# Sums as a column of ones among the values, in an attention and experts kernel

## The chip, the core and the metric

The kernel runs on one core of a Trainium2 chip. The metric is the device time of one execution in microseconds, the median of several runs.

## The reference

Two stages follow each other. The first is attention with 32 memory slots per head; the second sends each token to one of eight experts.

```python
# 8 batches, 8 heads, 576 tokens, head size 64, 32 slots; all float32
a = exp(phi - max_over_tokens(phi)); a = a / (sum_over_tokens(a) + 1e-9)
k_m = einsum('bhsm,bhsd->bhmd', a, k)          # memory keys
v_m = einsum('bhsm,bhsd->bhmd', a, v)          # memory values
attn = softmax(q @ k_m.T / 8); x = attn @ v_m  # 4608 tokens of 512
logits = x @ w_gate + modality_bias[modality_id]
e = argmax(logits); g = softmax(logits)[e]
out = g * (relu(x @ w1[e]) @ w2[e])            # 512 -> 1024 -> 512
```

The sum over tokens of `a`, one number for each head and slot, is what the change works out in another way.

## The kernel before

**Staging.** The kernel guesses one expert from the modality bias and computes all tokens with it. A verdict at the end (`verdict`, line 741) tells whether any token preferred another; only then a second part (`again`, line 1317, a branch on a register) does the work for all experts. With these inputs the branch skips it. The eight batches are worked off in turn, two of them to a pair. The value side of attention is folded into the first expert matrix: `value_products` (line 750) multiplies memory values by `w1`, `hidden` (814) multiplies the attention weights by that, `relu` (827 and 831) brings the result back in two parts, high and low, and `outputs` (850) does the second expert matrix in 24 matmuls of 512 columns for each tile of 128 tokens. `gated` (863) scales a tile on ACT into one of two `ob` buffers, and `store` sends it out from SP's queue.

**The memory of a batch.** `mem_max` to `mem_peak` find the maximum of phi, `mem_exp` (385 and 388) subtracts it on DVE and takes exponentials on ACT in two parts. From batch 1 on, `mem_sums` adds the nine token columns of the exponentials on GpSimd in a tree of four additions (`fold`, lines 311 to 315), and `kv_products` multiplies the exponentials by keys and values: 72 products of 64 rows, 32 columns of weights and 128 moving columns (64 of keys, 64 of values), in 144 instructions on tiles of the array, and one more product of the sums with `sides` (line 425), which adds over partitions. `kv_divide` divides on ACT, `mem_turn` turns keys and values for the next steps. Batch 0 has its own path (`first_products`, `first_sums`), with its sums on DVE.

**Loads.** Keys and values of a batch lie side by side in `kv_sb`, each loaded with one DMA in runs of 2,304 bytes. `more_keys`, behind the memory product, issues the next batch's. `load_queries` issues 16 DMAs in runs of 128 bytes. Nearly all DMAs go out from SP's queue, in order.

**The order.** Every engine executes its instructions in the order in which the code emits them. `weave` (line 1207) works that order out when the kernel is built: a list of attention stages, each with a due time, is woven into a list of expert stages. `TAKES` holds planned durations for each kind of stage (PE first, then a chain of engines such as "D0.4 A0.6"), `progress` counts expert work in about microseconds, and a stage is emitted once its predecessors are planned to be done and progress has reached its due time. Attention stages are strictly in order of due time. For the sums there is an allowance:

```python
t = max([0.0] + [done[n] + (0.1 if n[0] != "sums" else -1.2) for n in s[0][2] if n[0] != "g"])
```

The due times that matter here, after the start of a batch's memory work: `exp` 3.0, `sums` 3.2, the four query transpositions 5.6 to 8.6, logits of the batch before and `kv` at `MEMORY` (6.0), `kvT` 9.0.

**The end.** The last tile is evicted in halves, one on ACT and one on DVE, and stored with four DMAs, two from SP and two from ACT. Then each engine loads the verdict into a register (`values_load`, line 1408) and branches (line 1318).

Of the kernel before, what the change touches and what calls it, by code (L numbers as in the profile page):

```python
# [54 lines left out]
def attn_moe(ctx: ExitStack, tc: tile.TileContext, q, k, v, phi, mod_id, w_gate, mod_bias, w1, w2, out):  # L55
# [23 lines left out]
    BUSY = 145, 9  # L79
# [24 lines left out]
    sides = const.tile([P, NG], F32, name="sides")  # L104
# [25 lines left out]
    kv_sb = big.tile([P, 2, HG, QC * D], F32, name="kv_sb")  # L130
# [3 lines left out]
    raw2 = kv_sb.rearrange("p t j x -> p (t j x)")[:, 0:FCH * DM].rearrange("p (c d) -> p c d", d=DM)  # L134
# [28 lines left out]
    def warm_small(n):  # L163
        idle = pair_of_banks(0)
        for n in range(n):
            r, c = QP * (n % 2), BL * (n // 2 % 4)
            nc.tensor.matmul(
                idle[c:c + BL, n % 2, 0:16], lhsT=busy[r:r + QP, 0:BL], rhs=busy[r:r + QP, 0:16],
                start=True, stop=True, tile_position=(r, c),
            )  # L170
# [7 lines left out]
    def load_kv(b, t):  # L178
        nc.sync.dma_start(kv_sb[:, t], halves((k, v)[t], b))
# [128 lines left out]
    def fold(eng, src, op, name, where):  # L308

        t2 = wk.tile([P, HG, 4 * M], F32, name="t2" + where)  # L310
        eng.tensor_tensor(t2, src[:, :, 0:4 * M], src[:, :, 4 * M:8 * M], op=op)
        eng.tensor_tensor(t2[:, :, 0:2 * M], t2[:, :, 0:2 * M], t2[:, :, 2 * M:4 * M], op=op)
        r = wk.tile([P, HG, M], F32, name=name, bufs=2 if name == "sums" else 1)
# [12 lines left out]
    def mem_max(b):  # L326
        live["top", b] = fold(nc.vector, phs[b % 2], ALU.max, "top", "top")
# [39 lines left out]
    def mem_exp(b):  # L367
# [21 lines left out]
        live["pe", b] = pe, None  # L389

    def mem_sums(b):
        pe = live["pe", b][0]
        if b == 0:
            x = pe.rearrange("p j x -> p (j x)")
            n = QC // 3 * P
            t2 = wk.tile([P, HG, 4 * M], F32, name="t2top").rearrange("p j x -> p (j x)")[:, 0:n]
            r = wk.tile([P, HG, M], F32, name="sums", bufs=2)
            rf = r.rearrange("p j m -> p (j m)")
            nc.vector.tensor_tensor(t2, x[:, 0:n], x[:, n:2 * n], op=ALU.add)
            nc.vector.tensor_tensor(t2, t2, x[:, 2 * n:3 * n], op=ALU.add)  # L400
            nc.vector.tensor_tensor(rf, t2[:, 0:P], t2[:, P:2 * P], op=ALU.add)
            nc.vector.tensor_tensor(rf, rf, t2[:, 2 * P:3 * P], op=ALU.add)
            live["pe", b] = pe, r
            return
        live["pe", b] = pe, fold(nc.gpsimd, pe, ALU.add, "sums", "sums")
        if b > 1 and b + 2 < B:
            load_phi(b + 2)

    def kv_products(b):


        pe, sums = live["pe", b]
# [12 lines left out]
        nc.tensor.matmul(live["psum"], lhsT=sums.rearrange("p j m -> p (j m)"), rhs=sides, start=True, stop=True)  # L425

    def first_products(t):
# [9 lines left out]
        for c in range(QC):  # L437
            for j, g, half in tiles:
                nc.tensor.matmul(  # L439
                    to[g][M * j:M * (j + 2), 0:2 * D].rearrange("p (j d) -> p j d", j=2),  # L440
                    lhsT=pe[half, c, j:j + 2].rearrange("p j m -> p (j m)"), rhs=kv_sb[half, t, j:j + 2, c * D:(c + 1) * D],
                    start=(c == 0), stop=(c == QC - 1), tile_position=(QP * g, M * j),
                )
# [52 lines left out]
    def kv_divide(b):  # L496
# [6 lines left out]
        for g in range(NG):  # L503
            nc.scalar.activation(both[:, :, g], live["kvp"][:, g], AF.Copy, scale=rec[:, g])
        live["both", b] = both

    def more_keys(b):
        if b == 0:
            load_kv(1, 0)
            load_kv(1, 1)  # L510
            load_queries(1)
            load_modalities()
        elif b == 1:
            load_phi(2)
            load_phi(3)
        if 0 < b < B - 1:
            load_kv(b + 1, 0)
            load_kv(b + 1, 1)
# [23 lines left out]

    def mem_gate(b):
        pg = bank("pe" if b > 1 else "pa")
# [202 lines left out]


# [117 lines left out]
    def store(b, t):  # L866
# [6 lines left out]
        def finish(po):  # L873
            if b == B - 1 and t is None:
                parts = []
                for n, eng in enumerate((nc.sync, nc.scalar)):
                    ob = wk.tile([P, DM], F32, name="ob", bufs=2)
                    cols = slice(DM // 2 * n, DM // 2 * (n + 1))
                    if n:
                        nc.vector.tensor_scalar(ob[:, cols], po[:, cols], gate_of(b, t), None, op0=ALU.mult)  # L880
                    else:
                        nc.scalar.activation(ob[:, cols], po[:, cols], AF.Copy, scale=gate_of(b, t))
                    parts.append((eng, ob, cols))
# [21 lines left out]
    def first_w2(c):  # L905
# [44 lines left out]
    def plan_memory(b, due, floor=0.0):  # L950
# [6 lines left out]
        for name, after, what, late in (  # L957
# [3 lines left out]
            ("sums", [("exp0" if b < 2 else "exp", b)], mem_sums, 3.2),  # L961
            ("kv", [("exp0" if b < 2 else "exp", b), ("sums", b)], mem_kv, 6.0),
# [99 lines left out]
    def plan_steps(b, dues):  # L1062
# [46 lines left out]
        if b > 1:  # L1109
            add(("l", b), "lx", [("n", b, 1, 2), ("s", b, 0)] + ([("exp", b + 1), ("sums", b + 1)] if b + 1 < B else []), logits, b)  # L1110
# [80 lines left out]
    FIRST, AHEAD, SPREAD, MEMORY, LATE = 26.5, (1.4, 4.0), 0.55, 6.0, 4  # L1191
# [87 lines left out]
    with tc.manual_schedule():  # L1279
# [15 lines left out]
        nc.gpsimd.memset(sides, 0.0)  # L1295
        for g in range(NG):
            nc.gpsimd.memset(sides[QP * g:QP * (g + 1), g:g + 1], 1.0)
# [109 lines left out]
    why = "one or zero, worked out on the chip"  # L1407
    again(nc.values_load(bad_i[0:1, 0:1], min_val=0, max_val=P, skip_runtime_bounds_check_because=why))
# [28 lines left out]
```

## Time and profile before

| | us |
|---|---|
| median of 3 runs | 387.86 (387.04 to 390.87) |
| the profiled execution | 387.67 |
| its span, first to last instruction | 385.9 |
| PE busy | 373.8 |
| VectorE (DVE) busy | 247.7 |
| ScalarE (ACT) busy | 140.1 |
| GpSimd (POOL) busy | 47.4 |

The difference between the profiled execution's time and its span, 1.8 us, lies before the first and behind the last instruction. The mean granted clock of TensorE was 0.994. PE stands for matmuls and PEld for weight loads, which overlap them; a q behind an engine (ACTq, SPq) is its sequencer, which issues DMAs and does register work. Ends of matmuls are modelled, so starts are the better guide. An L with a number is a line of the kernel before.

### The profile page before, as it was taken

The page shows a single profiled execution, that of the slowest core. Times are in us where ns is not written, and L with a number is a line of the kernel's source. Part 1 is how long each engine was busy: PE and PEld are TensorE (multiplying, and loading weights), DVE is VectorE, ACT ScalarE, POOL GpSimd, SP SyncE. Part 2 cuts the span into 40 slices and gives each one's busy share as a digit, 9 for nine tenths or more (in the row PEclk, how much of TensorE's full clock was granted, in tenths as well). Part 3 has the DMA queues.
Part 4 walks back from the last instruction along what each step waited for, and adds up shares of the span by engine and source line. Part 5 has one row for each costly group of instructions (what it writes and reads, how often), then busy time and mean ns, then how long its engine had stood idle before and what let it go on. Part 6 is the DMA issues. An engine that isn't in the chain of part 4 may idle for free.

```text
span 385.9 us, 9650 instructions
## 1 busy us (share of the span) xinstructions
PE 373.8 (97%) x3878; PEld 304.4 (79%) x3879; DVE 247.7 (64%) x620; ACT 140.1 (36%) x327; POOL 47.4 (12%) x123
## 2 busy tenths in 40 slices
PE   7899999999999999999999999999999999999992
PEld 3577886879769887987879887887968877888981
DVE  4786756796688568856776468865796458850400
ACT  2382424515245235423443234331543225341310
POOL 4237050023000300030000300030000300000000
PEclk9999999999999999999999999999999999999997
DMA  8998679794951594729601395607001000420011
GB/s 297 376 400 196 72 132 336 166 303 127 291 126 29 161 252 98 279 63 296 128 27 56 76 304 107 278 24 273 32 27 54 3 29 27 189 114 35 23 56 34
DMA packets 94762, 56.87 MB, mean 147 GB/s; under 512 B 72564, under 2 KB 77940, under 8 KB 94708
## 3 DMA queue, kind: packets, MB, share of 16 engines
q1 hardware_dynamic: 94272, 55.74, 48.1%
q8 instruction: 32, 0.52, 0.5%
q10 hardware_dynamic: 436, 0.43, 0.4%
q14 instruction: 22, 0.18, 0.2%
HBM read 37.28 MB, written 18.87 MB: 146 GB/s over the span
## 4 chain that ended last, share of the span: by engine, by line
PE 90%; DVE 5%; ACT 2%; DMA 1%; issue 1%; ACTq 0%; POOL 0%; DVEq 0%; POOLq 0%
PE pe L850 50%; PE pe L814 26%; PE pair L420 4%; PE pair L568 2%; PE pe L757 2%; PE pair L757 1%; PE pair L703 1%; DMA row<-n_moe_modality_bias_dram 1%; PE pair L584 1%; PE pair L425 1%; PE pair L149 1%; PE pe L439 1%; DVE a L623 1%; DVE a L617 0%; DVE mx L621 0%
## 5 line engine op out<-in xcount | busy, mean ns | idle before, releaser
L850 PE MATMUL pe<-w2h,hh 128*128 128x512 f32 x288 | 115.6, 401 | 0.0
L850 PE MATMUL pe<-w2h,hl 128*128 128x512 f32 x288 | 112.4, 390 | 0.0
L850 PE MATMUL pe<-w2l,hh 128*128 128x512 f32 x288 | 110.1, 390 | 0.0
L831 DVE SCALAR_TENSOR_TENSOR hl<-pe,hh 128x256 fp32r<-128x256 f32 (+2 forms) x158 | 58.0, 391 | 37.4 <-ACT hh L827 36.5
L850 PEld LDWEIGHTS pe<-w2h,hh 128*128 128x128 f32 x288 | 54.1, 188 | 16.4 <-ACT vwh L154 4.2
L827 ACT ACTIVATE hh<-pe 128x256 fp32r<-128x256 f32 (+2 forms) x158 | 53.4, 363 | 36.9 <-PE pe L814 36.4
L850 PEld LDWEIGHTS pe<-w2l,hh 128*128 128x128 f32 x288 | 54.0, 188 | 11.6
L850 PEld LDWEIGHTS pe<-w2h,hl 128*128 128x128 f32 x288 | 54.2, 188 | 9.6
L863 ACT ACTIVATE ob<-pe,gates 128x512 f32<-128x512 f32 x35 | 24.0, 689 | 79.0 <-PE pe L850 37.8
L814 PE MATMUL pe<-xbh,vwh 128*128 128x320 f32 x128 | 39.9, 312 | 0.1
L814 PE MATMUL pe<-xbl,vwh 128*128 128x320 f32 x128 | 39.6, 309 | 0.0
L814 PE MATMUL pe<-xbh,vwl 128*128 128x320 f32 x128 | 39.6, 309 | 0.0
L814 PE MATMUL pe<-xah,vwh 128*128 128x256 f32 x124 | 35.2, 287 | 0.6 <-ACT xah L683 0.4
L814 PE MATMUL pe<-xal,vwh 128*128 128x256 f32 x124 | 35.0, 284 | 0.3 <-DVE xal L686 0.3
L814 PE MATMUL pe<-xah,vwl 128*128 128x256 f32 x124 | 34.9, 283 | 0.0
L354 POOL COPY ts<-tm 32x4 f32<-32x4 f32 x24 | 4.8, 200 | 184.4 <-DVE tm L346 183.6
L814 PEld LDWEIGHTS pe<-xah,vwh 128*128 128x128 f32 x124 | 23.5, 191 | 3.1 <-ACT xah L683 1.3
L814 PEld LDWEIGHTS pe<-xbh,vwh 128*128 128x128 f32 x128 | 24.0, 188 | 0.7 <-ACT ob L863 0.4
L814 PEld LDWEIGHTS pe<-xbl,vwh 128*128 128x128 f32 x128 | 24.1, 188 | 0.3
L814 PEld LDWEIGHTS pe<-xal,vwh 128*128 128x128 f32 x124 | 23.6, 191 | 0.8 <-DVE xal L686 0.5
L814 PEld LDWEIGHTS pe<-xbh,vwl 128*128 128x128 f32 x128 | 24.0, 188 | 0.0
L814 PEld LDWEIGHTS pe<-xah,vwl 128*128 128x128 f32 x124 | 23.6, 191 | 0.0
(184 smaller groups left out, 438.2 us busy)
## 6 DMA issues: line engine op xcount, KB each, us to landing
kv_sb<-in_k_dram SPq DMA_DIRECT2D x8, 1152.0 KB, 5.9
kv_sb<-in_v_dram SPq DMA_DIRECT2D x8, 1152.0 KB, 9.1
q_sb<-in_q_dram SPq DMA_DIRECT2D x112, 72.0 KB, 2.4
out_dram<-ob SPq DMA_DIRECT2D x28, 256.0 KB, 2.7
ph<-in_phi_dram SPq DMA_DIRECT2D x7, 576.0 KB, 4.2
raw<-in_moe_w_dram SPq DMA_DIRECT2D x2, 1024.0 KB, 6.2
out_dram<-ob SPq DMA_DIRECT2D x14, 128.0 KB, 2.3
raw<-in_moe_w_dram SPq DMA_DIRECT2D x1, 1280.0 KB, 10.0
```

The lines of the kernel that those rows point to most:

```text
L149: nc.tensor.transpose(dst, src, ident[:rows, :rows])
L354: nc.gpsimd.tensor_copy(ts_[BL * a:BL * (a + 1)], live["tm"][BL * o:BL * (o + 1)])
L420: nc.tensor.matmul(live["kvp"][M * j:M * (j + 1), g], lhsT=pe[half, j, c * M:(c + 1) * M], rhs=kv_sb[half, :, j, c * D:(c + 1) * D], start ...
L425: nc.tensor.matmul(live["psum"], lhsT=sums.rearrange("p j m -> p (j m)"), rhs=sides, start=True, stop=True)
L439: nc.tensor.matmul(to[g][M * j:M * (j + 2), 0:2 * D].rearrange("p (j d) -> p j d", j=2), lhsT=pe[half, c, j:j + 2].rearrange("p j m -> p ( ...
L568: nc.tensor.matmul(sc[g][M * j:M * (j + 1), a, 0:QC * BL].rearrange("p (c t) -> p c t", t=BL), lhsT=kvTs[b][half, 0, j], rhs=qT[half, j, a ...
L757: nc.tensor.matmul(pvs[g][M * j:M * (j + 1), :], lhsT=vT[b][rows, j, :], rhs=raw1[rows, j, cols], start=True, stop=not more, tile_position ...
L814: nc.tensor.matmul(ph[:, 0:n], lhsT=(vl if k == 2 else vh)[:, g, cols], rhs=xl if k == 1 else xh, start=(g == k == 0), stop=(g == NG - 1 a ...
L827: nc.scalar.activation(hs[0][:, f, h0:h0 + p1 - p0], live["ph", f][:, p0:p1], AF.Relu)
L831: nc.vector.scalar_tensor_tensor(hl, live["ph", f][:, p0:p1], 0.0, hh.bitcast(F32), op0=ALU.max, op1=ALU.subtract)
L850: nc.tensor.matmul(po, lhsT=tile_columns(hl if n == 1 else hh, f, t), rhs=(w2l if n == 2 else w2h)[:, f, :], start=(f == n == 0), stop=(f ...
L863: nc.scalar.activation(ob, po, AF.Copy, scale=gate_of(b, t))
```

## The change

The sums come out of the memory product itself. Each 64 values in `kv_sb` are followed by a one, set by one GpSimd memset ahead of batch 1's loads; the moving operand becomes two runs of 65 numbers, keys (with one number too many, which nobody reads) and values with their one, so that column 129 of the result is the sum. GpSimd's tree, `sides` and the product of line 425 go. Values from batch 1 on are loaded with four DMAs, in runs of 64 numbers. The load of phi two batches ahead is issued behind the exponentials. In the plan the memory product and the logits follow the exponentials alone, the product is planned at 2.3 for 2.6, and `MEMORY` is 7.4 for batches 3 to 7. Batch 1's gate becomes eight products on tiles of 64 rows, with 14 small filler products. The last tile is evicted by ACT alone and stored with two DMAs. The verdict is loaded into the registers during the last tiles.

```diff
-    BUSY = 145, 9
+    BUSY = 145, 9, 14
...
-    sides = const.tile([P, NG], F32, name="sides")
...
-    kv_sb = big.tile([P, 2, HG, QC * D], F32, name="kv_sb")
+    ks = QC * D
+    kv_sb = big.tile([P, HG, ks + QC * (D + 1)], F32, name="kv_sb")
+    with_ones = kv_sb[:, :, ks:].rearrange("p j (c e) -> p j c e", e=D + 1)
...
     def load_kv(b, t):
-        nc.sync.dma_start(kv_sb[:, t], halves((k, v)[t], b))
+        src = halves((k, v)[t], b)
+        if b == 0 or t == 0:
+            nc.sync.dma_start(kv_sb[:, :, ks * t:ks * (t + 1)], src)
+            return
+        for j in range(HG):
+            nc.sync.dma_start(with_ones[:, j, :, 0:D], src[:, j].rearrange("p (c d) -> p c d", d=D))
...
         live["pe", b] = pe, None
+        if 1 < b < B - 2:
+            load_phi(b + 2)
...
-        live["pe", b] = pe, fold(nc.gpsimd, pe, ALU.add, "sums", "sums")
-        if b > 1 and b + 2 < B:
-            load_phi(b + 2)
+    def keys_and_values(half, j, c):
+
+        x = kv_sb[half, j, c * D:c * D + D + 1]
+        return bass.AP(tensor=x.tensor, offset=x.offset, ap=[list(x.ap[0]), [ks + c, 2], [1, D + 1]])
...
-        pk = pair_of_banks(1)
-        live["psum"] = pk[:, 0, 2 * D:2 * D + NG]
-        live["kvp"] = pk[:, :, 0:2 * D].rearrange("p g (t d) -> p g t d", t=2)
+        pk = pair_of_banks(1)[:, :, 0:2 * (D + 1)]
+        live["psum"] = pk[:, :, 2 * D + 1]
+        live["kvp"] = pk.rearrange("p g (t e) -> p g t e", t=2)
...
-                        rhs=kv_sb[half, :, j, c * D:(c + 1) * D],
+                        rhs=keys_and_values(half, j, c),
...
-        nc.tensor.matmul(live["psum"], lhsT=sums.rearrange("p j m -> p (j m)"), rhs=sides, start=True, stop=True)
...
     def more_keys(b):
         if b == 0:
+            nc.gpsimd.memset(with_ones[:, :, :, D], 1.0)
             load_kv(1, 0)
...
+    def second_gate():
+
+        pg = pair_of_banks(0)
+        for j in range(HG):
+            for g in range(NG):
+                half = slice(QP * g, QP * (g + 1))
+                nc.tensor.matmul(
+                    pg[M * j:M * (j + 1), g, 0:E], lhsT=vT[1][half, j], rhs=wgd[half, j, g],
+                    start=True, stop=True, tile_position=(QP * g, M * j),
+                )
+        small_products(BUSY[2], pg[:, :, QP:QP + 16])
+        nc.vector.tensor_copy(vg[0][:, :, E:2 * E], pg[:, :, 0:E])
...
+    def count_bad():
+        why = "one or zero, worked out on the chip"
+        live["bad"] = nc.values_load(bad_i[0:1, 0:1], min_val=0, max_val=P, skip_runtime_bounds_check_because=why)
...
             if b == B - 1 and t is None:
-                parts = []
-                for n, eng in enumerate((nc.sync, nc.scalar)):
-                    ob = wk.tile([P, DM], F32, name="ob", bufs=2)
-                    cols = slice(DM // 2 * n, DM // 2 * (n + 1))
...
-                for eng, ob, cols in parts:
-                    for i in range(2):
-                        eng.dma_start(last(b - 1 + i)[:, cols], ob[QP * i:QP * (i + 1), cols])
+                ob = gated(b, t, po)
+                for i, eng in enumerate((nc.sync, nc.scalar)):
+                    eng.dma_start(last(b - 1 + i), ob[QP * i:QP * (i + 1)])
                 return
...
-            ("sums", [("exp0" if b < 2 else "exp", b)], mem_sums, 3.2),
-            ("kv", [("exp0" if b < 2 else "exp", b), ("sums", b)], mem_kv, 6.0),
+            ("kv", [("exp0" if b < 2 else "exp", b)], mem_kv, MEMORY if b > 2 else 6.0),
...
+            stage(attention, ("bad",), "nothing", [("v",)], count_bad, due=due + 28.0)
...
-    FIRST, AHEAD, SPREAD, MEMORY, LATE = 26.5, (1.4, 4.0), 0.55, 6.0, 4
+    FIRST, AHEAD, SPREAD, MEMORY, LATE = 26.5, (1.4, 4.0), 0.55, 7.4, 4
```

## Rows read from the trace of the kernel before

**Rows 1.** Page, part 1: engine, busy us (share of the span), instructions.

```profile
PE 373.8 (97%) x3878; PEld 304.4 (79%) x3879; DVE 247.7 (64%) x620; ACT 140.1 (36%) x327; POOL 47.4 (12%) x123
```

**Rows 2.** Stages: window, length, busy us of PE PEld DVE ACT POOL, clock, DMA.

```profile
14.00:31.00 17.00, 15.59 (x232) 10.59 (x240) 13.28 (x33) 12.32 (x30) 7.82 (x15) 1.00 1.04 390
...
200.00:250.00 50.00, 50.00 (x482) 41.87 (x481) 34.44 (x82) 18.61 (x39) 3.67 (x9) 1.00 0.51 152
...
378.60:385.90 7.30, 0.00 (x0) 0.00 (x0) 0.48 (x1) 0.47 (x1) 0.00 (x0) 0.70 0.18 45
```

**Rows 3.** The chain that ended last: start us, us, what.

```profile
54.45 2.24 PE pair L420 x140
...
217.64 2.18 PE pair L420 x144
219.82 0.31 PE pair L425 x2
220.13 1.50 PE pe L850 x6
```

**Rows 4.** Timeline of PE at batch 7's memory product: start us, us, instruction.

```profile
308.78 0.38 PE L425 MATMUL pair<-sides,sums 128*128 128x2 f32 x2
...
309.02 0.47 PE L850 MATMUL pe<-w2h,hh 128*128 128x512 f32 x1
```

**Rows 5.** Timeline of GpSimd (POOL); in brackets idle time before, and its releaser.

```profile
15.64 0.41 POOL L257 CAST mid_f<-mid 64x4 f32<-64x4 int32 x2 [8.09 <-DMA mid<-in_moe_modality_id_dram]
...
217.99 0.46 POOL L315 TENSOR_TENSOR sums<-sums,exp 128x128 f32<-128x128 f32 x1
```

**Rows 6.** Timeline of ScalarE (ACT), 38 to 125 us.

```profile
50.86 1.26 ACT L388 ACTIVATE exp<-exp 128x640 f32<-128x640 f32 x2 [1.29 <-DVE exp L385]
...
58.34 0.69 ACT L863 ACTIVATE ob<-pe,gates 128x512 f32<-128x512 f32 x1
...
88.53 0.67 ACT L863 ACTIVATE ob<-pe,gates 128x512 f32<-128x512 f32 x1
```

**Rows 7.** Timeline of PE: the fillers at the start, and batch 1's gate.

```profile
1.31 1.34 PE L167 MATMUL pair<-busy 64*32 64x16 bf16 x145 [1.31 <-POOL busy L1285]
...
70.37 0.26 PE L546 MATMUL pair<-wgd,kvT 128*32 128x16 f32 x8
```

**Rows 8.** SP's queue: start us, us of issue, DMAs in a row.

```profile
20.49 1.76 SPq L179 DMA_DIRECT2D kv_sb<-in_v_dram  x1
...
44.50 8.99 SPq L192 DMA_DIRECT2D q_sb<-in_q_dram  x16
53.58 3.62 SPq L895 DMA_DIRECT2D out_dram<-ob  x4
...
78.23 1.11 SPq L895 DMA_DIRECT2D out_dram<-ob  x2
```

**Rows 9.** Line 895, stores: us from issue to landing.

```profile
DMA to landing us min/median/max: 2.3/2.9/3.5
```

**Rows 10.** Timeline of the end, ACT, DVE and ACT's queue.

```profile
373.18 0.69 ACT L863 ACTIVATE ob<-pe,gates 128x512 f32<-128x512 f32 x1 [4.75 <-PE pe L850]
...
378.62 0.47 ACT L882 ACTIVATE ob<-pe,gates 128x256 f32<-128x256 f32 x1 [4.75 <-PE pe L850]
...
379.13 0.48 DVE L880 TENSOR_SCALAR ob<-pe,gates 128x256 f32<-128x256 f32 x1 [15.79 <-ACT ob L882]
379.64 1.19 ACTq L886 DMA_DIRECT2D out_dram<-ob  x2
```

**Rows 11.** Line 1408, register loads: ns min/median/max, first and last start us.

```profile
L1408 PEldq TENSOR_LOAD <-bad_i x1: 607/607/607, 374.3 to 374.3; - x1
...
L1408 ACTq TENSOR_LOAD <-bad_i x1: 864/864/864, 380.9 to 380.9; - x1
```

**Rows 12.** Line 1318, the branch on the verdict, ACT's sequencer.

```profile
L1318 ACTq EVENT_SEMAPHORE  x2: 17/17/17, 384.6 to 384.7; - x2
...
L1318 ACTq COMPARE_BRANCH  x1: 54/54/54, 381.8 to 381.8; - x1
```

More of the change, by code (lines that the diff above doesn't have):

```diff
@@ L163, in warm_small, with small_products @@
     def warm_small(n):
-        idle = pair_of_banks(0)
+        small_products(n, pair_of_banks(0)[:, :, 0:16])
+    def small_products(n, idle):
         for n in range(n):
@@ L167, in warm_small @@
             nc.tensor.matmul(
-                idle[c:c + BL, n % 2, 0:16], lhsT=busy[r:r + QP, 0:BL], rhs=busy[r:r + QP, 0:16],
+                idle[c:c + BL, n % 2], lhsT=busy[r:r + QP, 0:BL], rhs=busy[r:r + QP, 0:16],
                 start=True, stop=True, tile_position=(r, c),
@@ L305, in two_banks, with fold @@
         return [bank("pe") for _ in range(NG)]
-    def fold(eng, src, op, name, where):
-        t2 = wk.tile([P, HG, 4 * M], F32, name="t2" + where)
+    def fold(eng, src, op, name):
+        t2 = wk.tile([P, HG, 4 * M], F32, name="t2" + name)
         eng.tensor_tensor(t2, src[:, :, 0:4 * M], src[:, :, 4 * M:8 * M], op=op)
         eng.tensor_tensor(t2[:, :, 0:2 * M], t2[:, :, 0:2 * M], t2[:, :, 2 * M:4 * M], op=op)
-        r = wk.tile([P, HG, M], F32, name=name, bufs=2 if name == "sums" else 1)
+        r = wk.tile([P, HG, M], F32, name=name)
         eng.tensor_tensor(r, t2[:, :, 0:M], t2[:, :, M:2 * M], op=op)
@@ L326, in mem_max @@
     def mem_max(b):
[L327 removed]
+        live["top", b] = fold(nc.vector, phs[b % 2], ALU.max, "top")
     def mem_top(b):
@@ L389, in mem_exp @@
         live["pe", b] = pe, None
+        if 1 < b < B - 2:
+            load_phi(b + 2)
     def mem_sums(b):
         pe = live["pe", b][0]
[L393 to L404, printed above, removed]
-        live["pe", b] = pe, fold(nc.gpsimd, pe, ALU.add, "sums", "sums")
-        if b > 1 and b + 2 < B:
-            load_phi(b + 2)
+        x = pe.rearrange("p j x -> p (j x)")
+        n = QC // 3 * P
+        t2 = wk.tile([P, HG, 4 * M], F32, name="t2top").rearrange("p j x -> p (j x)")[:, 0:n]
+        r = wk.tile([P, HG, M], F32, name="sums")
+        rf = r.rearrange("p j m -> p (j m)")
+        nc.vector.tensor_tensor(t2, x[:, 0:n], x[:, n:2 * n], op=ALU.add)
+        nc.vector.tensor_tensor(t2, t2, x[:, 2 * n:3 * n], op=ALU.add)
+        nc.vector.tensor_tensor(rf, t2[:, 0:P], t2[:, P:2 * P], op=ALU.add)
+        nc.vector.tensor_tensor(rf, rf, t2[:, 2 * P:3 * P], op=ALU.add)
+        live["pe", b] = pe, r
+    def keys_and_values(half, j, c):
+        x = kv_sb[half, j, c * D:c * D + D + 1]
+        return bass.AP(tensor=x.tensor, offset=x.offset, ap=[list(x.ap[0]), [ks + c, 2], [1, D + 1]])
     def kv_products(b):
-        pe, sums = live["pe", b]
-        pk = pair_of_banks(1)
-        live["psum"] = pk[:, 0, 2 * D:2 * D + NG]
-        live["kvp"] = pk[:, :, 0:2 * D].rearrange("p g (t d) -> p g t d", t=2)
+        pe = live["pe", b][0]
+        pk = pair_of_banks(1)[:, :, 0:2 * (D + 1)]
+        live["psum"] = pk[:, :, 2 * D + 1]
+        live["kvp"] = pk.rearrange("p g (t e) -> p g t e", t=2)
         for c in range(QC):
@@ L440, in first_products @@
                     to[g][M * j:M * (j + 2), 0:2 * D].rearrange("p (j d) -> p j d", j=2),
-                    lhsT=pe[half, c, j:j + 2].rearrange("p j m -> p (j m)"), rhs=kv_sb[half, t, j:j + 2, c * D:(c + 1) * D],
+                    lhsT=pe[half, c, j:j + 2].rearrange("p j m -> p (j m)"), rhs=kv_sb[half, j:j + 2, ks * t + c * D:ks * t + (c + 1) * D],
                     start=(c == 0), stop=(c == QC - 1), tile_position=(QP * g, M * j),
@@ L503, in kv_divide @@
         for g in range(NG):
-            nc.scalar.activation(both[:, :, g], live["kvp"][:, g], AF.Copy, scale=rec[:, g])
+            nc.scalar.activation(both[:, :, g], live["kvp"][:, g, :, 0:D], AF.Copy, scale=rec[:, g])
         live["both", b] = both
@@ L541, in first_values @@
         nc.scalar.copy(vT[0].rearrange("p j m -> p (j m)"), pv[:, 0:P])
+    def second_gate():
[9 more added lines that the diff above has]
+        nc.vector.tensor_copy(vg[0][:, :, E:2 * E], pg[:, :, 0:E])
     def mem_gate(b):
-        pg = bank("pe" if b > 1 else "pa")
+        if b == 1:
+            second_gate()
+            return
+        pg = bank("pe" if b else "pa")
         for j in range(HG):
@@ L1109, in plan_steps @@
         if b > 1:
-            add(("l", b), "lx", [("n", b, 1, 2), ("s", b, 0)] + ([("exp", b + 1), ("sums", b + 1)] if b + 1 < B else []), logits, b)
+            add(("l", b), "lx", [("n", b, 1, 2), ("s", b, 0)] + ([("exp", b + 1)] if b + 1 < B else []), logits, b)
         c0, n = RA * i, RB if i else RA
@@ L1294, in attn_moe @@
         nc.gpsimd.memset(ones_c, 1.0)
-        nc.gpsimd.memset(sides, 0.0)
-        for g in range(NG):
-            nc.gpsimd.memset(sides[QP * g:QP * (g + 1), g:g + 1], 1.0)
         nc.gpsimd.memset(mid_f[:, 0], 0.0)
@@ L1405, in any_experts @@
                         outputs(None, range(FCH), scatter(2 * pair + 1, None, idx8[:, i, pair:pair + 1]))
-    why = "one or zero, worked out on the chip"
-    again(nc.values_load(bad_i[0:1, 0:1], min_val=0, max_val=P, skip_runtime_bounds_check_because=why))
+    again(live["bad"])
 _INS = ["q", "k", "v", "phi", "moe_modality_id", "moe_w_gate", "moe_modality_bias", "moe_w1", "moe_w2"]
```

7 lines of the change are left out of this document (1 added, 6 removed), and 2 rows, old and new, of the table TAKES.

## The prediction

> **What bounds the kernel now.** I read the page's engine shares first: TensorE (PE) is busy 373.8 us, 97% of the span [rows 1]. Shares are an average, so the next view is the busy time by stage. From 200 to 250 us PE is busy all 50.00 us at a granted clock of 1.00; the last 7.30 us hold no PE work at all; and between 14 and 31 us the DMA engines are saturated, 390 GB/s at a share of 1.04 [rows 2]. So three places decide: what PE executes in the steady batches, what follows its last matmul, and whether the early loads, which leave no room, start to hold somebody up. The critical chain tells what a memory product costs PE: 144 matmul instructions in 2.18 to 2.24 us, then 0.31 us for the two instructions that multiply GpSimd's sums [rows 3]. Where PE works the clock stands at its upper level, 2.4 GHz [rows 2], so no term below is for the clock.
>
> **The sums leave PE.** Seven batches (1 to 7) lose the product of line 425. The chain charges it 0.31 us [rows 3]; in the timeline it starts at 308.78 and the next matmul starts at 309.02, 0.24 us later [rows 4]. The change of tile shape after line 420 stays whatever follows, so the gain lies between 7 x 0.24 = 1.7 and 7 x 0.31 = 2.2 us; I take 1.9, the middle. In return each of the 72 products has 130 columns in place of 128. If time goes by columns, that is 2/128 of 2.18 us, 0.034 us a batch, 0.24 in all; if the instructions are bound by their issue, nothing. I take 0.2.
>
> The tree of four adds on GpSimd goes too. Its last add began at 217.99, behind the start of the memory product at 217.64 [rows 3, 5], so it set how early the product could be placed. The order is computed when the kernel is built: the product was released 1.2 us ahead of the planned end of sums that take 2.9 us, that is 1.7 us behind the exponentials. Now it is released 0.1 us behind them. By the planner's output step of 0.69 us it moves two steps, some 1.4 us, forward. Does PE then wait for the exponentials? In batch 1 the product began at 54.45 [rows 3]; two steps earlier is about 53.1, and ACT's exponentials ended at 50.86 + 1.26 = 52.12 [rows 6]. One microsecond of cover is left, so this is costed at nothing; were the cover gone, the wait would be paid once a batch. The later due time (7.4 for 6.0) puts one more query transposition ahead of the logits. It hardly holds the logits back: worked through with the planner's own figures, they were released by the sums, over five units past their due time in batch 2. PE executes the same instructions in another order, and I give the order itself nothing.
>
> The memset of ones stands in GpSimd's queue ahead of a copy that waited 8.09 us for a transfer until 15.64 [rows 5]; the memset can run when the first value products end, near 14, so it costs nothing.
>
> **The gate of batch 1.** Eight instructions taking 0.26 us [rows 7] become sixteen on smaller tiles, plus 14 filler products. The sixteen at the memory product's 2.18/144 = 15 ns come to 0.24 us, and the fillers at 1.34 us/145 = 9 ns [rows 7] to 0.13. Against 0.26, that is +0.1; the bounds are 0 and +0.3, should the shape change drain the array. Queued behind it is only PE's next hidden product.
>
> **The values in short runs.** From batch 1 on, each load of values has 4,608 pieces of 256 B where it had 512 of 2,304 B, in four DMAs. No row shows such pieces. The nearest: sixteen query loads of 72 KB, in pieces of 128 B, were issued over 8.99 us [rows 8], so 0.98 ns a piece; long pieces move at 390 GB/s [rows 2], 3.0 us for the 1.18 MB. If a piece costs what a 128-byte piece costs, the new load takes 4.5 us; if bytes go at the queries' rate, 9.0. A line through both prices gives 1.27 ns a piece, 5.8 us, which I take since 256 B lies nearer to 128 than to 2,304: +2.8 us of transfer (bounds +1.5 and +6.0). In the steady batches nobody waits: the values are used a batch later. The early stage is different. From 20.49 us SP's queue runs back to back through values, 16 query loads and others to the first four stores at 53.58, and again to the stores at 78.23 [rows 8]. Whatever the loads of batches 1 and 2 add, these stores are late by. Behind a late store waits `gated` on ACT, which needs one of two `ob` buffers. The first two stores land 2.9 us after issue [rows 9], near 57, and ACT took the buffer at 58.34 [rows 6]. At +2.8 it waits until about 60. In the new order the turned keys precede it on ACT, and the next thing PE needs of ACT is the upper half of the value weights, near 61: hidden. The second place is the store at 78.23, landing near 82, whose buffer ACT took at 88.53 [rows 6, 8, 9]. Two loads at +2.8 make 87.6: still hidden, by about half a microsecond once PE is a little earlier. I cost the loads at nothing and keep up to 6 us for the range.
>
> The Trainium skill's page "DMA: Bandwidth & Descriptors" (section Specifications) speaks against this edit: it asks for at least 512 B a transfer for full rate. The trace bears the direction out in the rates just named. The same page (section "Why small descriptors are slow (HBM only)") counts 11 cycles where 8 carry data for 256 B; by that figure alone an estimate of the load is 4.1 us, +1.1, and the sum would be the same.
>
> **The end.** Before: ACT evicts half a tile at 378.62, VectorE the other half only at 379.13, after ACT, and ACT issues two DMAs from 379.64 for 1.19 us [rows 10]. Then ACT loads the verdict's register in 0.864 us [rows 11], branches in 0.054, and is next seen at 384.6 [rows 12]; the span ends 1.3 us later. The 2.7 us between branch and next instruction I take as the price of the branch, which stays. After: one eviction of 0.69 us [rows 10] from 378.62 to 379.31 in place of 379.61 (-0.30), one DMA issue in place of two (-0.6), no register load (-0.9): -1.8 us. The other path that must end is the landing of the last store, 2.9 us [rows 9] behind 379.4, at 382.3, plus SP's bookkeeping; ACT now comes out at about 382.8. They lie close together, hence bounds of -1.2 and -1.9. By their due time the register loads move to twenty output steps (13.6 us) before the end. PE's took 0.607 us at 374.3, while its matmuls held ACT's last eviction back to 378.62 [rows 10, 11], so its sequencer was 4 us ahead: hidden. ACT and VectorE idle for microseconds between tiles there; SP merely delays a store that nobody awaits. If the sequencer's lead were gone, the load would cost 0.6.
>
> **Sum.** -1.9 + 0.2 + 0.1 - 1.8 = -3.4 us. The profiled execution took 387.67 us, 1.8 of them outside its span; it becomes 384.3. The median of the runs stands 0.19 higher, so 384.5. With all terms at their ends, 383.8 to 385.5.
>
> **The rivals.** *The short runs hold up PE (the slower side).* If bytes move at the queries' rate, each of the two early loads adds 6.0 us. The first delays the buffer of 58.34 past 63, the value weights follow, and PE loses about 2 us. After the second, the store of 78.23 lands near 94, 6 us behind 88.53; ACT stands there with the relus of the hidden products queued behind it, and since four PSUM banks cover little over 1.4 us, PE loses 4.5. Net -3.4 + 6.5: 391.0. It begins to cost when a load adds more than about 3.1 us. SP's saturated queue speaks for it; against it, the line through both prices stays below that point. A milder form, 2 us lost, gives 386.5.
>
> *The keys and values are read more slowly.* The two runs of 65 numbers start on odd addresses. If TensorE fetched whole 16-byte lines and were bound by it, 65 numbers would touch 17 or 18 lines where 64 touched 16: 8% of 2.18 us, 0.18 a batch, 1.2 in all: 385.7. With eight products side by side a column costs 2.18 x 8 / 144 / 128 = 0.95 ns, against 1.50 / 6 / 512 = 0.49 on line 850 [rows 3]; a stream at half speed hints that reading isn't the limit. The Trainium skill's page "SBUF — State Buffer" (section "Door 1: The DMA port swizzle") states such 16-byte lines; no row here shows them.
>
> *The end doesn't give.* If the last landing or the barrier sets the end, only the eviction and part of an issue are won, 0.6: 385.7.
>
> *More comes back than the sum has.* ACT evicts a tile right ahead of batch 1's split at 67 us, and PE idles about 1 us there. Should the earlier scores let the split go first, another microsecond: 383.5. By the planner's times it misses that place narrowly.
>
> **Chances.** Forecast 0.55; loads hold up PE 0.18 (the full price 0.07, the mild form 0.11); slower reading 0.07; no gain at the end 0.08; more back 0.12. Within the forecast the terms' bounds leave some three in ten below 384.0, one per cent under 387.86, about what a measurement of this kernel can tell. Faster by over 1%: 0.55 x 0.3 + 0.10 = 0.27, which I set at 0.3; slower by over 1% (over 391.7) needs the full price and more: 0.05; within 1%: 0.65. The range, with one in ten out at each end: 382.9 to 388.4.
>
> **What would show it.** No product with sums, GpSimd's adds gone; the memory product no longer than 2.25 us; PE busy all of 200 to 250; SP's stores of 53.58 and 78.23 later by about 3 and 5 us, with no idle PE after 58 and 88; ACT's last event near 382.8 and the span near 382.5. Wrong would be a PE gap beside a waiting `gated`, a product above 2.4 us, or a PE gap at the early register load.

## The result, and the profile after

The changed kernel takes 390.38 us (median of 14 runs, 389.55 to 392.76) where the kernel before takes 388.0 (14 runs): a ratio of 1.0056, 95% interval 1.0032 to 1.0079. The prediction was 384.5, range 382.9 to 388.4.

The profiled execution took 391.94 us, 1.6 above its median; e12_again below is a second trace of the same kernel at 390.14, and what both show is told first. Line numbers are those of the changed kernel: outputs 880 (850 before), hidden products 844 (814), memory products 430 (420), `gated` 893 (863), value load 187, stores 916.

The page's engine shares, which answer to [rows 1], show GpSimd's adds gone and PE busy a little longer:

```profile
PE 375.0 (96%) x3886; PEld 304.3 (78%) x3887; DVE 248.1 (64%) x619; ACT 141.2 (36%) x327; POOL 26.4 (7%) x93
```

The early stage decides. SP's queue, to be held against [rows 8] (start us, us of issue):

```profile
18.70 2.36 SPq L184 DMA_DIRECT2D kv_sb<-in_k_dram  x1
31.31 3.90 SPq L187 DMA_DIRECT2D kv_sb<-in_v_dram  x4
35.26 12.08 SPq L200 DMA_DIRECT2D q_sb<-in_q_dram  x16
...
51.18 9.75 SPq L200 DMA_DIRECT2D q_sb<-in_q_dram  x16
61.02 3.06 SPq L916 DMA_DIRECT2D out_dram<-ob  x4
...
65.42 0.45 SPq L184 DMA_DIRECT2D kv_sb<-in_k_dram  x1
72.95 5.86 SPq L187 DMA_DIRECT2D kv_sb<-in_v_dram  x4
78.91 1.84 SPq L916 DMA_DIRECT2D out_dram<-ob  x2
...
89.66 1.11 SPq L916 DMA_DIRECT2D out_dram<-ob  x2
```

Between 21.06 and 31.31 SP issues nothing, and again from 65.9 to 72.95. Its waits name the reason (total us, times, longest); SP's queue in the kernel before has no such row:

```profile
SPq L187 <- DMA kv_sb<-in_k_dram: 44.8, 7, 10.2
```

Each batch's values wait until its keys have landed. Keys and values of a head row now lie side by side in one tile, a load of values writes nine runs with gaps, and the program orders it behind the keys' load although they share no byte (e16_wait and e17_nowait below test that the place alone decides). So the first four stores start at 61.02 in place of 53.58. The next two pairs are later still: 78.91 and 89.66 answer to these rows of the kernel before, so the store of 78.23, the second place of the prediction, is 11.4 us late (10.0 in the second trace) and not 5:

```profile
60.39 1.11 SPq L895 DMA_DIRECT2D out_dram<-ob  x2
...
78.23 1.11 SPq L895 DMA_DIRECT2D out_dram<-ob  x2
```

What stands behind the first four is seen on ScalarE, beside [rows 6] (in brackets the idle time before, and what ended it):

```profile
65.01 0.69 ACT L893 ACTIVATE ob<-pe,gates 128x512 f32<-128x512 f32 x1 [5.84 <-DMA out_dram<-ob]
65.59 1.07 ACT L155 CAST vwh<-pe 128x512 fp32r<-128x512 f32 x2
66.54 0.65 ACT L651 ACTIVATE a<-a 128x512 f32<-128x512 f32 x1
...
70.15 0.62 ACT L709 CAST xah<-aT 128x512 fp32r<-128x512 f32 x1 [1.08 <-DVE aT L675]
...
93.70 0.69 ACT L893 ACTIVATE ob<-pe,gates 128x512 f32<-128x512 f32 x1 [1.04 <-DMA out_dram<-ob]
...
123.96 0.69 ACT L893 ACTIVATE ob<-pe,gates 128x512 f32<-128x512 f32 x1 [2.78 <-DMA out_dram<-ob]
```

The gating waits 5.84 us for a store to land. Queued behind it on ScalarE are the value weights, the exponentials of batch 1's scores, and through VectorE the split `xah` at 70.15, which PE's hidden products need. The second trace shows the same; on PE's timeline

```profile
70.72 0.38 PE L844 MATMUL pe<-xah,vwh 128*128 128x256 f32 x1 [2.78 <-ACT xah L709]
```

where the kernel before had 0.39 us of idle time at the same product, and in the second trace's stages around that (window, length, busy us of PE PEld DVE ACT POOL, granted clock, DMA):

```profile
68.00:70.00 2.00, 0.00 (x0) 0.00 (x0) 1.87 (x5) 0.00 (x0) 0.00 (x0) 1.00 1.08 389
...
72.00:74.00 2.00, 2.00 (x42) 1.75 (x41) 2.00 (x5) 0.77 (x2) 0.00 (x0) 0.69 0.27 104
74.00:76.00 2.00, 2.00 (x11) 2.00 (x11) 0.60 (x3) 0.39 (x1) 0.00 (x0) 0.50 0.65 144
```

After the idle stretch the granted clock falls to 0.50, the 1.2 GHz level, where in the kernel before it stood at 1.00 (68 to 70 and 72 to 76 us). In the second trace the 89th hidden product is 2.6 us late, and 1.4 more are gone by the 113th, mostly at the lower clock. PE's 121st hidden product starts 4.08 us later than before in the first trace and 4.03 in the second. From there on the second gains: at its last output product it is 2.92 us late. The first is 4.72 us late there. It stood idle twice more behind late gatings, those of 93.70 and 123.96 above; PE's timeline has

```profile
94.44 0.41 PE L844 MATMUL pe<-xbh,vwh 128*128 128x320 f32 x1 [0.72 <-ACT ob L893]
...
124.70 0.39 PE L844 MATMUL pe<-xah,vwh 128*128 128x256 f32 x1 [0.65 <-ACT ob L893]
```

The steady batches are what was forecast, 50.00 us of 50.00 busy, and in each of the last five the matmul after the memory product starts 2.22 us behind the product's start, where it was 2.42 with the sums:

```profile
310.07 2.29 PE L430 MATMUL pair<-kv_sb,exp 64*32 64x130 f32 x144
312.29 0.50 PE L880 MATMUL pe<-w2h,hh 128*128 128x512 f32 x1
```

The end answers to [rows 10 to 12]: ScalarE's timeline, and the line of the branch on the verdict (ns min/median/max, first and last start us):

```profile
383.34 0.69 ACT L893 ACTIVATE ob<-pe,gates 128x512 f32<-128x512 f32 x1 [4.75 <-PEq L1336]
384.06 0.55 ACTq L907 DMA_DIRECT2D out_dram<-ob  x1
```

```profile
L1336 SPq EVENT_SEMAPHORE  x9: 17/17/17, 387.9 to 388.5; - x9
...
L1336 ACTq EVENT_SEMAPHORE  x2: 17/17/17, 387.9 to 388.0; - x2
...
L1336 SPq COMPARE_BRANCH  x1: 53/53/53, 384.6 to 384.6; - x1
L1336 ACTq COMPARE_BRANCH  x1: 54/54/54, 384.6 to 384.6; - x1
```

From the end of PE's last product (383.25) to the span's end (390.15) it is 6.90 us, in both traces, where it was 7.35: 0.45 us gained.

So the second trace says: +4.0 us in the early stage, -1.1 after that, where the sums are gone, -0.45 at the end. That is +2.5, and the medians say +2.4. The first trace has a further 1.8 us, nearly all from the two late gatings at 94 and 124 us. It also lost 1.3 us by 47 us, told in the last section, but these aren't part of the 1.8: at the 121st hidden product the two traces stand level, since in both the landing of the same store released the gating, at 65.0 and 64.9 us.

### The profile page after: what moved, and what is told of

The parts are those of the page before. It is cut to its first block, busy times and chain, and to the rows that moved or that the text cites. A ratio compares the mean times of both kernels' runs of the same rounds, so it can differ in the third digit from the quotient of the medians.

```text
span 390.2 us, 9625 instructions
## 1 busy us (share of the span) xinstructions
PE 375.0 (96%) x3886; PEld 304.3 (78%) x3887; DVE 248.1 (64%) x619; ACT 141.2 (36%) x327; POOL 26.4 (7%) x93
## 5 line engine op out<-in xcount | busy, mean ns | idle before, releaser
L583 DVE STREAM_TRANSPOSE q_sb<-q_sb 128x576 f32<-128x576 f32 (+2 forms) x32 | 23.2, 758 | 0.0
```

Of the source, the lines that this page charges most:

```text
L583: nc.vector.transpose(x, x)
```

## The experiments

Theory 1: the values' wait for the keys' landing holds up SP, so that stores, gating and PE are late. Theory 2, the prediction's rival: the 256-byte runs themselves take the time. Theory 3: the end gives 0.4 us and not 1.8. Theory 4: the 1.3 us that the first trace had lost by 47 us belong to VectorE and GpSimd.

| kernel | us | ratio to before, 95% interval |
|---|---|---|
| changed kernel | 390.38 | 1.0032 to 1.0079 |
| e1_apart | 387.55 | 0.9956 to 0.9992 |
| e2_mixed | 388.78 | 0.9988 to 1.0035 |
| e3_short_runs | 391.67 | 1.0053 to 1.0116 |
| e4_end | 386.92 | 0.9942 to 0.9975 |
| e6_stores | 386.28 | 0.9938 to 0.9973 |
| e7_both | 386.48 | 0.9940 to 0.9978 |
| e8_due | 387.62 | 0.9968 to 0.9997 |
| e9_short_stores | 389.40 | 1.0023 to 1.0050 |
| e10_end_stores | 389.52 | 1.0005 to 1.0051 |
| e11_halves | 391.61 | 1.0082 to 1.0114 |
| e13_stores_only | 389.59 | 0.9982 to 1.0050 |
| e16_wait | 395.43 | 1.0165 to 1.0214 |
| e17_nowait | 389.70 | 1.0029 to 1.0059 |

**e1_apart: the wait taken away, the short runs kept.**

```diff
-    kv_sb = big.tile([P, HG, ks + QC * (D + 1)], F32, name="kv_sb")
+    kv_sb = big.tile([P, HG * (ks + QC * (D + 1))], F32, name="kv_sb")
...
```

All keys lie first in it, then all values.

> The changed kernel with one thing undone: the keys of all head rows lie together and the values with their ones behind them, so that no byte of the keys' region lies between bytes of the values'; short runs, four value loads, ones column, order and end stay. Theory 1 (the values' loads wait on SP for the landing of the keys' load, 10.2 us in all over three batches, since their regions interleave, and hold up the stores behind them): PE is no longer late by 2.7 to 5.5 us in 68 to 132 us, and the time falls by about 4, to 386.0 to 387.0. Theory 2 (the short runs themselves take the time): it stays at 389.5 to 391. Theory 4 (the 1.3 us that are lost by 47 us are VectorE's and GpSimd's work at 33 us): they stay lost under either.

387.55 us, 2.8 less than the changed kernel and now 1.0 below before, if not the 386 to 387 expected (where 10.2 us, the longest of the seven waits, stands for the sum of three). The stores of batch 0 start at 57.56, still 4.0 later than before, the gating waits a little and PE isn't held up by it. Why the stores stay late shows on SP's queue, where the short runs hold up the issue of the values without any wait (1.76 us in [rows 8]); the gating's wait is on ScalarE's timeline:

```profile
21.28 10.98 SPq L188 DMA_DIRECT2D kv_sb<-in_v_dram  x4
```

```profile
60.76 0.69 ACT L894 ACTIVATE ob<-pe,gates 128x512 f32<-128x512 f32 x1 [1.79 <-DMA out_dram<-ob]
```

**e2_mixed: the wait alone, in the kernel before.** `kv_sb` becomes `[P, HG, 2, QC * D]`, the loads unchanged.

> The kernel before with one thing changed: keys and values of a head row lie side by side, so that their regions interleave and the values' one load must wait for the keys' landing; runs of 2304 bytes, sums, order and end as before. Theory 1: slower than before, by 2 to 4.5 us (390 to 392.5), with a wait of 2 to 4 us per batch on SP ahead of the value load and later stores. Theory 2: as before, 387.5 to 388.5.

388.78, no difference, but it tested nothing: its trace has no wait on the keys. Here both loads write patterns of one stride; that this is why no wait arises is likely and not shown. e16_wait took its place.

**e16_wait and e17_nowait: the same four loads with and without the wait.** Runs of 768 bytes with gaps of 16, in the kernel before; only the place of the keys differs.

```diff
+for j in range(HG):
+    nc.sync.dma_start(spaced[:, j, :, 0:3 * D], src[:, j].rearrange("p (c d) -> p c d", d=3 * D))
```

> The kernel before with the values of batches 1 to 7 in four loads of 768-byte runs with gaps of 16 bytes, beside the keys of their head row, so that here the wait of the values for the keys' landing does arise; sums, order, end and queues as before. Theory 1 in its plain form (the wait alone makes the stores late enough): stores of batch 0 at 58 us or later in place of 53.58, the gating waits for them, 389.5 to 391. If the wait only hurts together with 256-byte runs: stores before 57 us, no gating waits, within 1 us of e17_nowait.

> The same kernel with the keys of all head rows together and the values behind them: the same four loads of 768-byte runs without the wait. Theory 1: as before, 387.3 to 388.7, with the stores of batch 0 at 53 to 55 us.

395.43 against 389.70: the wait alone costs 5.7 us, more than was expected and more than the changed kernel lost. Theory 1 stands in its plain form. Rows of e16_wait: SP's wait,

```profile
SPq L186 <- DMA kv_sb<-in_k_dram: 45.0, 7, 9.4
```

ScalarE's timeline,

```profile
62.10 0.69 ACT L875 ACTIVATE ob<-pe,gates 128x512 f32<-128x512 f32 x1 [3.53 <-DMA out_dram<-ob]
62.69 0.36 ACT L542 COPY kvT<-pair 128x256 f32<-128x256 f32 x1
```

PE's timeline,

```profile
63.10 1.49 PE L580 MATMUL pair<-q_sb,kvT 64*32 64x288 f32 x11 [3.34 <-ACT kvT L542]
```

and the stage behind it:

```profile
64.00:68.00 4.00, 4.00 (x46) 2.14 (x35) 1.96 (x4) 0.33 (x1) 0.00 (x0) 0.50 1.09 381
```

The stores of batch 0 start at 58.96 (54.35 in e17_nowait). In the order of the kernel before, the copy of the turned keys stands behind the gating, so PE starves at once for 3.34 us and then works at the 1.2 GHz level. In the changed kernel the keys come first on ScalarE, as the prediction said, and the same lateness reaches PE only at `xah`. e17_nowait lies 1.6 us above before, not at it: 1.2 of the 2.1 us in its trace are lost by 25 us, where the granted clock falls to 0.50 (18 to 20 us) as in e1_apart (last section). The rest stays open.

**e3_short_runs: the short runs alone, in the kernel before; e9_short_stores: the same with the early stores on GpSimd's queue.**

> The kernel before with one thing changed: from the second batch on the values come in four loads of 256-byte runs with a gap of 4 bytes between them, keys and values apart, no ones read; sums, order and end as before. Theory 1: within 0.8 us of before (387.6 to 388.8). Theory 2: 390 to 392.

> The kernel of e3_short_runs (before, with the values in 256-byte runs) with the stores of batches 0 and 1 on GpSimd's queue. If its 3.2 us are the stores' lateness: 387.8 to 388.8, as before. If they are the loads themselves, or TensorE's own stall of 2.73 us that its profile shows in the midst of the products at 98.97 us: 390.5 to 392.

391.67 and 389.40. The first is the time that theory 2 gave, so in the order of the kernel before 256-byte runs do cost, 3.2 us, and not by late stores: no gating in e3_short_runs waits longer than 0.45 us. Its trace (396.0 us, 4.3 above its median) has PE standing still in the midst of a memory product, on nothing that the profile shows, and 1.3 us lost as in theory 4:

```profile
98.97 0.68 PE L433 MATMUL pair<-kv_sb,exp 64*32 64x128 f32 x15 [2.73 <-issue]
```

With the stores moved this standstill is gone and 1.5 us of loss remain; the 1.3 us of theory 4 are in that trace too. So short runs do harm in this kernel's old order by other ways than the stores; how much of it a standstill like this, or theory 4's loss, makes in the other runs is not settled.

**e6_stores and e7_both: the wait and the short runs kept, the early stores out of their way.** e6_stores is the changed kernel, e7_both is e1_apart, each with this edit:

```diff
+    def out_queue(b):
+        return nc.gpsimd if b < 2 else nc.sync
...
-                nc.sync.dma_start(out[S * b + P * t:S * b + P * (t + 1)], ob)
+                out_queue(b).dma_start(out[S * b + P * t:S * b + P * (t + 1)], ob)
```

The two other stores are changed likewise.

> The changed kernel with one thing moved: the stores of batches 0 and 1 are issued by GpSimd's queue and not by SP's, so that they no longer stand behind the loads of keys, values and queries. Wait and short runs stay. Theory 1 (the loss is the stores' lateness, which holds up the gating on ScalarE and so TensorE): 387 to 388, and no gating waits for a store's landing. Theory 2 (the packets themselves, or late keys and values): 389.8 to 391.

> The kernel of e1_apart with the stores of batches 0 and 1 on GpSimd's queue as well. If what the short runs still cost there is SP's time at issuing them (8 to 11 us per batch in place of 1.8): 384.5 to 386. If it is the packets' time on the DMA engines, or nothing: as e1_apart, 387.2 to 387.9.

386.28 and 386.48: 4.1 us come back, more than the 387 to 388 expected, and e6_stores beats both kernels. About 0.4 of the 4.1 lie at the end, where its trace has 6.54 us behind PE's last product for 6.90 (SP's branch, see e4_end); the rest is on PE. The values wait for the keys as in the changed kernel, only no store stands behind them. SP's wait, ScalarE's timeline and PE's in e6_stores:

```profile
SPq L187 <- DMA kv_sb<-in_k_dram: 43.1, 7, 9.9
```

```profile
58.51 0.69 ACT L893 ACTIVATE ob<-pe,gates 128x512 f32<-128x512 f32 x1 [0.38 <-PE pe L880]
```

```profile
68.64 0.39 PE L844 MATMUL pe<-xah,vwh 128*128 128x256 f32 x1 [0.32 <-ACT xah L709]
```

That shows the chain of theory 1 at its middle link: not late values, not the packets, but late stores. Taking the wait away as well (e7_both) adds nothing to the time, which lies between its two cases; its trace lost 1.1 us by 25 us at a granted clock of 0.50, which that of e6_stores didn't.

**e10_end_stores, e13_stores_only, e14_look, e15_look: is it the stores' move alone?** The same edit in the kernel before, with and without the new end; e14_look and e15_look repeat e10_end_stores.

> The kernel before with the end of the change and the stores of batches 0 and 1 on GpSimd's queue; sums, loads and order as before. It is what e6_stores is to be held against: what lies between them is the sums off TensorE with their short-run loads. If moving the stores is worth nothing to the kernel before, whose gating never waits for a store: as e4_end, 386.5 to 387.3. Sums worth 1.2 to 1.5 us by the steps of TensorE's delay in e6_stores would then leave e6_stores ahead by about that; a share of it lost to short runs leaves less.

> The kernel before with the stores of batches 0 and 1 on GpSimd's queue and nothing else. Its gating never waits for a store, so that by theory 1 there is nothing to gain: 387.3 to 388.7. If GpSimd's queue itself cost something, as half of the times of e10_end_stores (386.96 to 391.11) would have it: 389 to 391.

> The kernel of e10_end_stores once more, for a trace: its twelve times fall into 387.0 to 387.7 and 389.3 to 391.1, and its first trace is of the lower group. Of a trace of the upper group: 2 to 3 us more, either in TensorE's steps (its last product later than 378.6 us) or behind them (more than 7 us from its last product to the span's end). Theory 1 names neither.

> The same kernel a third time, as for e14_look: one of the two looks should fall into the upper group, if the groups come by chance at about even odds.

389.52 and 389.59, and 387.60 and 388.86 for the repeats: in the kernel before the move gains nothing, as theory 1 has it, and rather costs; 386.5 to 387.3 was expected with the end. Of that, 0.85 us lie behind PE's last product (6.95 us, 6.10 in e4_end). Its times spread from 387 to 391 (388 to 392.6 without the end, where the kernel before beside it went from 387.6 to 392.5). e15_look has PE idle 1.04 us on "issue" at 60.15 us, so part of the spread is of that kind; no trace of a run above 389 was had, and it stays open. What e6_stores wins isn't the move alone.

**e5_long_runs: no short runs, no sums at all.**

> The kernel of e1_apart without its short runs and its ones: each batch's values come in one load of 2304-byte runs, keys and values apart; the 65 columns stay, the 65th being whatever lies next, and the sums are left out altogether: the keys and values of batches 1 to 7 are divided by a constant. What is left of the change is the end, the order and the absence of the sums. If the short runs cost 3.2 us here as they did in e3_short_runs: 384.3. If they are hidden once the values don't wait for the keys: 387.3 to 387.8. If the sums are worth the 1.9 us of the prediction on top of the 1.5 us that e4_end showed for the end: 385.0.

1605 us: with the constant divisor the verdict comes out as one and the branch's body runs, so the time says nothing. The trace up to the branch does: its last output product starts at 376.83 us, before's at 378.14, e6_stores' at 377.51. By these single traces sums, gate and order together are worth 1.3 us on PE, and the short runs with their wait take 0.7 of it once the stores are out of the way.

**e4_end and e11_halves: the end.** e11_halves is e6_stores with this in place of the one eviction and two stores of 64 rows:

```diff
+                    both = bass.AP(tensor=x.tensor, offset=x.offset, ap=[[S * DM, 2], list(x.ap[0]), list(x.ap[1])])
+                    eng.dma_start(both, ob[:, cols])
```

ScalarE evicts the left half, which goes out from SP's queue; VectorE the right one, which goes out from ScalarE's.

> The kernel before with the end alone: ScalarE gates the whole last tile, one store on each of two queues, and the verdict's registers are loaded some 10 us earlier. As predicted, 1.8 us faster: 386.2. Theory 3 (what the trace of the changed kernel shows: 6.95 us from PE's last end to the span's end in place of 7.37, with both queues standing 3.2 us behind their branch): 387.4 to 387.8.

> The kernel of e6_stores with another last tile: ScalarE gates the left half of the columns and VectorE the right one, each stored by one store of its own queue. The half takes 0.47 us where the whole takes 0.69 us: 0.2 us faster, 386.1, if nothing else moves; equal within the measurement in any case.

e4_end: 386.92, a gain of 1.6 us (1.0 to 2.3) beside the 1.8 predicted; from PE's last product to the end it is 6.10 us in its trace. There SP meets its next instruction 0.45 us behind its branch, and only ScalarE takes 3.4:

```profile
L1314 SPq EVENT_SEMAPHORE  x9: 17/17/17, 380.9 to 382.9; - x9
...
L1314 ACTq EVENT_SEMAPHORE  x2: 17/17/17, 383.8 to 383.9; - x2
...
L1314 SPq COMPARE_BRANCH  x1: 53/53/53, 380.4 to 380.4; - x1
```

In the changed kernel both stand 3.3 us, and SP's row of semaphores (1.4 us, to 389.2) comes after that and not during it. SP's 0.44 us are found in the kernel before, e4_end, e6_stores and e7_both, its 3.3 us in the changed kernel, e1_apart, e8_due and e10_end_stores, alike in repeated traces. What decides between them stays open. e11_halves is 5.3 us slower than e6_stores, for a reason of its own (last section).

**e8_due and e12_again.**

> The kernel of e1_apart with the due time MEMORY set back from 7.4 to 6.0 (key-and-value products and logits of batches 3 to 7 earlier among the expert's products). The prediction took the order as worth nothing: 387.2 to 387.9. If the later logits give or cost something it shows as more than 0.7 us either way.

> The changed kernel once more, unchanged, for a second trace: whether the 1.3 us that VectorE's subtraction lost at 33.76 us (2.86 us for 1.60) belong to the change or to one execution. If to the change: 2.8 to 2.9 us again; if to the execution: 1.6 us. The wait of the values behind the keys and of the gating for stores must stand in either case.

387.62 beside 387.55 for e1_apart: no worth of the due time shows, as predicted. e12_again: 390.14, VectorE's subtraction 1.57 us, so the 1.3 us by 47 us belong to the execution; the wait (44.0 us, 7 times) and the gating's wait (7.17 us) are there again.

## Why the prediction was wrong

**The step that failed** is the one on the values in short runs: "Whatever the loads of batches 1 and 2 add, these stores are late by" was right in kind, and so was the way from a late store to `gated` and on to PE. (Not all of it arrives: in e1_apart the values' issue ends 10.0 us later than before and the stores start 4.0 later, since the queries between them are issued in 11.3 us for 17.2.) What the loads add was wrong, and so the cost of nothing that I gave them. I asked only how long the pieces take and took 2.8 us. Without the wait the stores of batch 0 were 3.1 us late (e3_short_runs) and 4.0 (e1_apart), so that term was mis-sized little, and PE didn't idle there, as forecast, though 4.0 is more than the cover of 3.1 us that the prediction allowed. What was left out was a new wait: the edit also moved keys and values into one region per head row, and I never asked what the values' load would have to wait for. With it the stores were 7.4 us late, 8.3 in the second trace, and that was beyond the cover. PE then stood idle for 2.78 us in the second trace and worked on at half the clock, where the prediction had no term for the clock. e16_wait prices that wait alone at 5.7 us, and e6_stores wins 4.1 back by freeing the stores from it. That isn't the whole distance to 384.5: e1_apart, without the wait, stands at 387.55, of which some 1.4 are the end (below), and 1.3 were lost in its trace by 25 us, where the granted clock fell at 18.

**The rival** "short runs hold up PE" named 391.0, close to the measured time, and the place, which is partly luck. Its cause was the runs' rate, and its chance was set by the line through two prices; the wait needs no slow bytes. It put 2 us at the first place and 4.5 at the second; 4.0 were lost at the first, and at the second 1.0 in one trace and nothing in the other. That short runs cost 3.2 us in the old order, by ways outside the stores, no case of mine had.

**The sums**: from 2.42 to 2.22 us per product in the last five batches, 0.20 net; in batches 1 and 2 from 2.48 to 2.22 and from 2.60 to 2.21, so 1.65 over seven. I had 0.27 less 0.034 per product, 1.7. For a steady batch the row of the timeline (0.24) and not the chain's (0.31) was the right end. The two extra columns cost 0.04 us a batch (2.18 to 2.22), as taken, and the odd addresses nothing beside that. That rival was priced too high in any case: 65 numbers of 4 bytes touch 17 lines of 16 bytes wherever they start, never 18.

**The gate, the order, the early register loads**: nothing visible. For the due time alone e8_due shows no difference; the register load at 366.3 us on PE's sequencer leaves no gap.

**The end**: the parts are as booked (e4_end has 1.6 us), yet in the changed kernel 0.45 came through. I took ScalarE's 2.7 us for the price of the branch and gave SP's path only a landing and its bookkeeping; each engine pays by itself, and SP, which paid 0.4 before, now paid 3.3. The signs that I named don't fit together either: ScalarE's last event "near 382.8" is counted from before's PE and leaves out the 1.6 us by which PE was to end earlier, the span "near 382.5" has them in.

## What to carry to other kernels

When data is laid out anew, ask of every load that writes there what it will now be ordered behind, not only how fast it moves; a wait on a queue is paid by whatever is queued behind it. Look in the trace for a wait whose releaser shares no byte with the waiter. Where a queue carries both loads with slack and stores whose buffers somebody waits for, give the stores another queue before tuning the loads, and measure it: in the kernel before, where nobody waited for a store, the same move gained nothing.

## What the runs showed of the hardware that was not expected

**PE stands still on "issue"**, for a time that varies between executions of like programs: 0.40 us at 16 us in the kernel before and 0.86 in e1_apart at the same place, both with the DMA engines full (shares 1.04 and 1.05), but 2.73 in e3_short_runs with the DMA engines all but idle (its stage from 96 to 98 us):

```profile
96.00:98.00 2.00, 0.24 (x18) 0.00 (x0) 0.00 (x0) 0.00 (x0) 0.00 (x0) 1.00 0.05 13
```

So full DMA engines don't explain it, and its cause is open. In e1_apart the granted clock falls after it, and 1.3 us are lost by 25 us (PE's timeline, then the stage):

```profile
16.70 0.81 PE L611 MATMUL pair<-q_sb,kT 32*32 32x128 f32 x36 [0.86 <-issue]
```

```profile
18.00:20.00 2.00, 1.84 (x24) 0.58 (x32) 1.91 (x5) 0.53 (x2) 1.26 (x4) 0.50 1.05 389
```

The length of the standstill doesn't decide that: the clock fell there in e1_apart, e7_both, e8_due and e17_nowait, behind 0.86, 0.50, 0.66 and 0.40 us, and not in e6_stores, behind 0.95.

**VectorE and GpSimd hold each other up, by about a whole instruction.** GpSimd's last splits of the weights run from 31.9 to 36 us, and VectorE's subtraction of two operands comes in between: 1.60 us in the kernel before, where GpSimd's last split then takes 1.93, but

```profile
33.76 2.86 DVE L649 TENSOR_TENSOR a<-a,mx 128x640 f32<-128x640 f32 x1
```

in the first trace of the changed kernel, where that split takes 1.32. The subtraction is longer by 1.26, about one split. Which goes first changes between executions of the changed kernel and moves PE by 1.3 us there. The Trainium skill's page "SBUF — State Buffer" (section "Terms") speaks of a port pair that the two share under a lock held for the full instruction; these rows agree. The long subtraction stands in three of the nineteen traces, all of kernels with 256-byte runs (e3_short_runs and e9_short_stores are the others); whether short runs make it likelier is open.

**A store over two places of 64 rows each, in one DMA, ran on few engines.** In e11_halves the two stores of 128 KB, issued from 378.05 us on, still ran at 386 us at a DMA share of 0.13; in e6_stores SP's store of 64 whole rows, 128 KB as well, landed 2.3 us after its issue. The stage in e11_halves:

```profile
380.00:386.00 6.00, 0.00 (x0) 0.00 (x0) 0.00 (x0) 0.00 (x0) 0.00 (x0) 0.66 0.13 42
```

The Trainium skill's page "DMA: Bandwidth & Descriptors" (section "Why a DMA increments its semaphore by 16 and not by 1") says that a DMA takes the largest number of engines up to 16 that divides the slowest dimension of both its sides. That is two here, and by it an estimate of the share is 2 of 16, 0.125; the trace's 0.13 agrees.
